# Second products three steps behind, each pass of a tile one tile later on ScalarE and VectorE, and an opening in single file

## The chip, the cores and the metric

The program runs on one core of a Trainium2 chip. The metric is the device time of one execution in microseconds (us); smaller is better. TensorE (PE) multiplies matrices into PSUM, ScalarE (ACT), VectorE (DVE) and GpSimd (POOL) work element by element, and SyncE (SP) issues most of the transfers. Each engine works through its own queue strictly in order, and engines meet only at semaphores.

## What is computed

The input is `x`, 4 sequences of 4096 tokens with 192 channels in float32. A causal convolution of 7 taps, whose weights are a softmax per head of 24 channels, gives 16384 tokens of 192 channels. Two layers of the same shape follow:

```python
x = attn_out.reshape(B * S, D)                 # after the convolution: 16384 x 192
h = x @ w_in;  g = h * np.cos(h);  x = g @ w_out      # first layer, 192 -> 2048 -> 192
h = x @ w_in2; g = np.where(h > 0, h, np.exp(np.minimum(h, 0)) - 1)
return g @ w_out2                                     # second layer
```

The weights of both layers arrive as float64 and are turned into pairs of 32-bit numbers on the chip, a high part and a low part; so are `x` and `g`. A product of two such pairs takes three products (high with high, low with high, high with low).

## The kernel before, in words

The tokens are cut into 32 blocks of 512. The unit of work is a step `(m, b, j)`: layer m, block b, and the j-th of 8 slices of 256 hidden channels. A step has two tiles, t = 2s and 2s + 1, each 128 hidden channels by 512 tokens. There are 512 steps. Blocks go in groups of four: 32 steps of the first layer for four blocks, then 32 of the second for the same four, eight times over.

Per step, TensorE does the first products of step s (`products_A`, 9 per tile, into a PSUM bank called `u`) and the second products of an earlier step s - LAG (`products_B`, 10 per tile, into the banks `acc`). Each uses half of the array's rows, and two run side by side: one stream is the 9 of the even tile and then 10 second products, the other 10 second products and then the 9 of the odd tile. So a step is 19 such pairs. While the second layer's weights are still being decoded, the second products of a step are 10 products on the whole array instead (`whole_B`), after the 9 pairs of first products; they need two `acc` banks and not four.

Between the two products each tile passes through the other engines: `emit_act1` (ACT reads `u`), `emit_mid` (DVE, first layer only), `emit_act2` (ACT, sine or exponential), `emit_g` (DVE, the last to read `u`, whose bank is then free), `emit_hi` (ACT, tile `gh`) and `emit_lo` (POOL, or DVE for odd tiles of the second layer, tile `gl`). `step(s)` writes these out by hand: each engine's queue has the order in which `step` calls them. The `u` banks form a ring: three while the weights are decoded, four afterwards.

At the end of a block, `half_evac` copies two of the four `acc` banks out on ACT and adds the other two on DVE (the next block's second products need the same banks), and `sums` finishes the block a piece at a time. `convs` gives one DVE instruction of a later block's convolution per half step of the second layer.

The opening is different. Weights are decoded by `decode` in four stages (load; ACT; DVE; POOL, then ACT and POOL once more), and `advance` moves pieces from stage to stage between the other instructions. All pieces use one PSUM bank, `brink`. The first two blocks go through the first layer side by side in 16 steps, block 1 two slices behind block 0 (SKEW); then come blocks 2 and 3.

Of the kernel before, what the change touches and what calls it, by code (L numbers as in the profile page):

```python
# [18 lines left out]
P = 128  # L19
# [4 lines left out]
SKEW = 2  # L24
LAG = 2
PAIR = 4
AWAKE = 14
RAW1, RAW2 = 4, 2
# [5 lines left out]
def conv_then_two_mlps(ctx, tc, x, weight, w_in1, w_out1, w_in2, w_out2, out):  # L34
# [40 lines left out]
    brink = ps_w.tile([P, N], F32, tag="t", name="t")  # L75
# [67 lines left out]
    zturn = {1: deque(range(ZN)), 2: deque(range(2, ZN))}  # L143

    def raw_tile(m):

        zturn[m].rotate(-1)
        t = zt.tile([P, 2 * N], I32, tag=f"zp{zturn[m][0]}", name="raw")
        return t.rearrange("p (n two) -> p n two", two=2)
# [7 lines left out]
    def decode(m, load, n):  # L157
# [5 lines left out]
        raw = raw_tile(m)[:, 0:n]  # L163
# [3 lines left out]
        t = brink[:, 0:n]  # L167
# [4 lines left out]
        size = w if scalar[0] else t  # L172
# [110 lines left out]
    XPS = {("a", 0): ("u0", "u1"), ("c", 0): ("u2", "b0"), ("c", 1): ("u0", "u1")}  # L283
# [4 lines left out]
    def bank(tag, name):  # L288
        return (ps_u if tag[0] == "u" else ps_a).tile([P, N], F32, tag=tag, name=name)
# [10 lines left out]
    def from_rows(what, b):  # L300
# [11 lines left out]
        ps = [bank(k, "xps") for k in XPS.get((what, b), ("b0", "b1"))]  # L312
        for o, k0, c, np in ((ps[0], KM, KH, 2 * Q), (ps[1], 0, KM, P)):
            cols = o[:, 0:np * c].rearrange("p (a k i) -> p k i a", k=c, i=Q)
            for k in range(c):
# [6 lines left out]
                nc.tensor.transpose(cols[0:D2, k], t[0:np, b % 2, k0 + k, P:D], ident[0:np, 0:np])  # L322
        yield
        H0 = HALO * Q
# [17 lines left out]
    def conv(what, b):  # L342
# [13 lines left out]
        o = yp.tile([P, N], F32, tag="y" + what, name="y", bufs=4 if what == "a" else 2)  # L356
# [103 lines left out]
    def split(b):  # L460
        if ("c", b) in ys:
            yield from split_pair(b)
        sh, sl, ch, cl = doubles(("sh", "sl")) + ready_x.pop(b) if b < 2 else doubles()
# [54 lines left out]
    def products_A(t):  # L518
# [4 lines left out]
        ops = [(k, w, h) for k in "cos" for w, h in (("h", "h"), ("l", "h"), ("h", "l"))]  # L523
# [17 lines left out]
    def whole_B(s):  # L541

        m, b, j = steps[s]
        if j == 0:
            acc[m, b] = [bank(f"{'ab'[b]}{k}", "acc") for k in (0, 1)]
# [9 lines left out]
    whole = {(1, 0), (1, 1)}  # L555
# [57 lines left out]
    def emit_hi(t):  # L613
        gh = wk.tile([P, N], F32R, tag="gh", name="gh", bufs=4)
# [3 lines left out]
    def emit_lo(t):  # L618
        gl = wk.tile([P, N], F32R, tag="gl", name="gl", bufs=4)
# [11 lines left out]
    def whole_evac(m, b):  # L631
        yield
        yield
# [7 lines left out]
        lazy.append(whole_z(b, z, c, e))  # L641
        yield

    def whole_z(b, z, c, e):
        lo, hi = half
        nc.vector.scalar_tensor_tensor(out=e[2][lo], in0=c[lo], scalar=TWO_PI, in1=e[3][lo], op0=ALU.mult, op1=ALU.add)
# [6 lines left out]
    def half_evac(m, b):  # L653
# [9 lines left out]
        yield  # L663
# [62 lines left out]
    raws = {1: RAW1, 2: RAW2}  # L726

    def fetch():
        while todo and len(loaded) + sum(len(stages[k]) for k in "12") < raws[todo[0][1]] and (todo[0][1] == 1 or moved):
# [22 lines left out]
    def need(m, at, *kinds):  # L752
        while any(ready.get((k, m), 0) < at for k in kinds):
            advance()

    def convs():
        for b in range(2, NBLK):
# [4 lines left out]
            while b - 4 not in split_done and b >= 4:  # L762
# [6 lines left out]
    conved, split_done = set(), set()  # L769
# [12 lines left out]
    begin_at = {max(s - (AHEAD, AHEAD2)[m - 1], 2 * NP - SKEW - 1 + 2 * (b - 2)): (m, b) for (m, b), s in first.items() if (m, b) not in whole}  # L782
# [8 lines left out]
    def step(s):  # L791
        now = 0 <= s < total
        if now:
# [8 lines left out]
        if ends:  # L802
            m, b = steps[s - LAG][:2]
            while not prepared and (m, b) == (1, 2):
                advance()
            assert not lazy
            finish = evac(m, b)
# [4 lines left out]
        for i in (0, 1):  # L812
# [15 lines left out]
            if not (ends and i) and (now and not first_mlp or s > 3 and ROWS - 1 not in conved and (i or 2 not in conved)):  # L828
# [116 lines left out]
```

## Time and profile before

| | |
|---|---|
| median of 3 runs | 2437.54 us (2435.3 to 2440.31) |
| the profiled execution | 2437.8 us, of which the span from first to last instruction is 2436.1 us |
| PE busy, weight loads busy | 96%, 77% of the span |
| ACT, DVE, POOL busy | 79%, 69%, 50% |
| granted TensorE clock, mean | 0.986 of full speed |

Busy shares are means over the whole program. An opening of some 265 us, in which weights are decoded, is followed by a long part that repeats itself for each group of four blocks, so a stretch of each is to be looked at by itself. The end of a matmul is modelled; the starts of successive matmuls tell how fast TensorE really goes.

### The profile page before, as it was taken

The numbers are of one execution on the slowest core, as the hardware profiler recorded it, in microseconds if no ns is written. First come the engines' busy times: TensorE is split into PE (matmuls) and PEld (weight loads), VectorE is DVE, ScalarE is ACT, GpSimd is POOL, SyncE is SP. The second block draws the span as 40 slices with busy tenths as digits, with TensorE's granted clock in tenths as the row PEclk, the third lists the DMA queues.
The fourth block names the chain that finished last, engine by engine and source line by source line (L and its number), as shares of the span: only waits on it lengthen the run. The fifth ranks groups of instructions, "written<-read, shape, count | busy, mean of one in ns | idle before, by whom it ended". The sixth has DMA issues, their size and how long they took to land.

```text
span 2436.1 us, 49759 instructions
## 1 busy us (share of the span) xinstructions
PE 2327.4 (96%) x19414; PEld 1884.4 (77%) x19414; DVE 1682.3 (69%) x2573; ACT 1926.9 (79%) x3426; POOL 1221.0 (50%) x975
## 2 busy tenths in 40 slices
PE   6777999999999999999999999999999999999998
PEld 4556877778888788777887788878888778877886
DVE  5776777667776686766776677666767668666654
ACT  4666878888888878878888888888888887887886
POOL 3665533664346633565336653366434663356532
PEclk8898999999999999999999999999999999999999
DMA  4233132111331022210331113211123102211011
GB/s 105 61 79 72 30 65 57 39 27 31 61 61 36 18 58 54 40 38 17 66 60 43 36 24 67 54 34 27 37 54 61 36 19 54 49 33 45 19 36 27
DMA packets 278876, 111.27 MB, mean 46 GB/s; under 512 B 231536, under 2 KB 245872, under 8 KB 278640
## 3 DMA queue, kind: packets, MB, share of 16 engines
q1 hardware_dynamic: 278192, 107.70, 20.9%
q8 instruction: 152, 2.49, 0.4%
q14 instruction: 84, 0.69, 0.1%
q10 hardware_dynamic: 448, 0.39, 0.1%
HBM read 29.91 MB, written 12.58 MB: 17 GB/s over the span
## 4 chain that ended last, share of the span: by engine, by line
PE 46%; DVE 23%; ACT 22%; issue 6%; POOL 2%; DMA 1%; SPq 1%; DVEq 0%; ACTq 0%; POOLq 0%
PE acc L563 24%; PE u L563 23%; ACT w L601 7%; DVE w L609 6%; ACT gh L615 6%; DVE w L595 5%; ACT w L586 3%; DVE w L611 3%; DVE gl L622 2%; DVE e L658 2%; DVE y L363 1%; POOL gl L622 1%; ACT w L603 1%; ACT e L659 1%; ACT e L660 1%
## 5 line engine op out<-in xcount | busy, mean ns | idle before, releaser
L622 POOL TENSOR_TENSOR gl<-w,gh 128x512 fp32r<-128x512 f32 x768 | 995.4, 1297 | 1153.1 <-ACT gh L615 890.4
L563 PE MATMUL acc<-gh,wo_hl 64*128 64x512 f32 x3968 | 1231.4, 391 | 15.5 <-DVE e L658 13.6
L615 ACT ACTIVATE gh<-w 128x512 fp32r<-128x512 f32 x1024 | 646.9, 632 | 216.5 <-DVE w L609 121.7
L563 PEld LDWEIGHTS acc<-gh,wo_hl 64*128 64x128 f32 x3968 | 719.5, 185 | 101.2 <-DVE e L658 26.9
L563 PE MATMUL acc<-gl,wo_hl 64*128 64x512 f32 x1984 | 773.4, 391 | 14.5 <-POOL gl L622 12.8
L563 PE MATMUL acc<-gh,wo_s 64*128 64x512 f32 x1984 | 773.9, 391 | 12.3 <-DVE e L658 11.1
L563 PE MATMUL acc<-gl,wo_s 64*128 64x512 f32 x1984 | 770.5, 389 | 0.0
L563 PE MATMUL u<-ch,wi_c 64*128 64x512 f32 x2048 | 645.1, 396 | 45.0 <-DVE w L609 32.9
L563 PE MATMUL u<-sh,wi_o 64*128 64x512 f32 x2048 | 627.1, 391 | 0.0
L609 DVE TENSOR_TENSOR w<-u,w 128x512 f32<-128x512 f32 x512 | 353.9, 691 | 357.6 <-ACT w L601 354.7
L611 DVE SCALAR_TENSOR_TENSOR w<-w,u 128x512 f32<-128x512 f32 x512 | 349.4, 682 | 212.4 <-ACT w L603 211.5
L563 PEld LDWEIGHTS u<-ch,wi_c 64*128 64x128 f32 x2048 | 373.5, 185 | 95.5 <-DVE w L609 38.0
L563 PE MATMUL u<-z,wi_o 64*128 64x512 f32 x1536 | 430.6, 386 | 0.0
L563 PEld LDWEIGHTS acc<-gl,wo_hl 64*128 64x128 f32 x1984 | 365.4, 185 | 71.5 <-POOL gl L622 36.7
L563 PEld LDWEIGHTS acc<-gh,wo_s 64*128 64x128 f32 x1984 | 365.3, 184 | 69.7 <-DVE e L658 33.0
L563 PEld LDWEIGHTS u<-sh,wi_o 64*128 64x128 f32 x2048 | 376.6, 187 | 37.4
L601 ACT ACTIVATE w<-w 128x512 f32<-128x512 f32 x512 | 323.7, 632 | 94.4 <-DVE w L595 89.3
L563 PE MATMUL u<-cl,wi_c 64*128 64x512 f32 x1024 | 395.9, 391 | 0.5 <-DMA cl<-z 0.5
L563 PE MATMUL u<-sl,wi_o 64*128 64x512 f32 x1024 | 395.3, 390 | 0.0
L563 PEld LDWEIGHTS acc<-gl,wo_s 64*128 64x128 f32 x1984 | 365.3, 185 | 33.6
L595 DVE SCALAR_TENSOR_TENSOR w<-u,w 128x512 f32<-128x512 f32 x512 | 348.7, 681 | 50.5 <-ACT w L586 49.9
L588 ACT ACTIVATE w<-u 128x512 f32<-128x512 f32 x512 | 303.9, 594 | 98.7 <-PE u L563 91.1
(123 smaller groups left out, 3413.9 us busy)
## 6 DMA issues: line engine op xcount, KB each, us to landing
out_dram<-e SPq DMA_DIRECT2D x192, 64.0 KB, 2.0
xa<-in_x_dram SPq DMA_DIRECT2D x112, 88.0 KB, 2.9
sh<-z SPq DMA_DIRECT2D x64, 128.0 KB, 2.4
sl<-z SPq DMA_DIRECT2D x64, 128.0 KB, 2.5
ch<-z SPq DMA_DIRECT2D x64, 128.0 KB, 2.4
cl<-z SPq DMA_DIRECT2D x64, 128.0 KB, 2.3
sh<-xh SPq DMA_DIRECT2D x62, 128.0 KB, 2.4
sl<-xl SPq DMA_DIRECT2D x62, 128.0 KB, 2.3
```

The lines of the kernel that those rows point to most:

```text
L363: nc.vector.scalar_tensor_tensor(out=o, in0=i, scalar=w, in1=o, op0=ALU.mult, op1=ALU.add)
L563: nc.tensor.matmul(o, lhsT=lhsT, rhs=rhs, start=first, stop=final)
L586: nc.scalar.activation(out=w.bitcast(I32), in_=u, func=AF.Copy, bias=0.25)
L588: nc.scalar.activation(out=w, in_=u, func=AF.Relu, scale=-1.0)
L595: nc.vector.scalar_tensor_tensor(out=w, in0=u, scalar=0.25, in1=w.bitcast(I32), op0=ALU.add, op1=ALU.subtract)
L601: nc.scalar.activation(out=w, in_=w, func=AF.Sin, scale=6.283185)
L603: nc.scalar.activation(out=w, in_=w, func=AF.Exp, scale=-1.0)
L609: nc.vector.tensor_tensor(out=w, in0=u, in1=w, op=ALU.mult)
L611: nc.vector.scalar_tensor_tensor(out=w, in0=w, scalar=-1.0, in1=u, op0=ALU.add, op1=ALU.max)
L615: nc.scalar.activation(out=gh, in_=wrk[t], func=AF.Copy)
L622: eng.tensor_tensor(out=gl, in0=wrk.pop(t), in1=f32(own[0]), op=ALU.subtract)
L658: add = lambda o, a: nc.vector.scalar_tensor_tensor(out=o, in0=a, scalar=scale, in1=o, op0=ALU.mult, op1=ALU.add)
```

## The change

Second products run three steps behind the first ones (LAG 3; `gh` and `gl` have six buffers each and not four). In `step`, each half step now calls `act1` and `mid` for tile t, `act2` and `g` for tile t - 1, and `hi` and `lo` for tile t - 2; before it was t, t and t - 1. Both additions of `half_evac` stand ahead of the odd tile's passes.

In the opening the blocks go one after another, each 8 steps. The ring has four `u` banks from the start; decoding has two banks (`brink` of two); the second products of the first blocks use the two banks `a0` and `a1`, and `b0`, `b1` are taken where the two decoding banks were once decoding is over. Up to three pieces move per step in the first 8 steps, and one per step later; the first layer's input weights come earlier in the order. The number of raw buffers follows from which of the four blocks' `z` tiles are still unused. The convolution's result of a block goes into the tile that later holds that block's `zc`, so the convolution of block b waits until block b - 4 has been doubled (`double_z`).

```diff
-SKEW = 2
-LAG = 2
+LAG = 3
-    brink = ps_w.tile([P, N], F32, tag="t", name="t")
+    brink = [ps_w.tile([P, N], F32, tag=f"t{k}", name="t") for k in range(2)]
+    def free_raws():
+        return [k for k in range(ZN) if present[0] < (k + 1) * NP + LAG - 4]
...
-        t = brink[:, 0:n]
+        brink.reverse()
+        t = brink[0][:, 0:n]
...
-        o = yp.tile([P, N], F32, tag="y" + what, name="y", bufs=4 if what == "a" else 2)
+        o = zt.tile([P, N], F32, tag=f"zc{b % ZN}", name="y") if what == "a" else yp.tile([P, N], F32, tag="yc", name="y")
...
-            blocks = list(range(b0, b0 + size))
-            if not steps:
-                steps += [(m, b, j - b * SKEW) for j in range(NP + SKEW) for b in blocks[0:2] if 0 <= j - b * SKEW < NP]
-                blocks = blocks[2:]
-            steps += [(m, b, j) for b in blocks for j in range(NP)]
+            steps += [(m, b, j) for b in range(b0, b0 + size) for j in range(NP)]
-    ring = deque((ps_u, f"u{k}") for k in range(3))
+    ring = deque((ps_u, f"u{k}") for k in range(4))
-    whole = {(1, 0), (1, 1)}
+    whole = set()
     def products(s):
         now, then = 0 <= s < total, 0 <= s - LAG < total
+        if then and steps[s - LAG][2] == 0 and not late:
+            whole.add(steps[s - LAG][:2])
-        gh = wk.tile([P, N], F32R, tag="gh", name="gh", bufs=4)
+        gh = wk.tile([P, N], F32R, tag="gh", name="gh", bufs=6)
-        gl = wk.tile([P, N], F32R, tag="gl", name="gl", bufs=4)
+        gl = wk.tile([P, N], F32R, tag="gl", name="gl", bufs=6)
     def half_evac(m, b):
...
         add(e[0], a0)
-        yield
         add(e[2], a1)
...
-            while b - 4 not in split_done and b >= 4:
+            while b >= ROWS and b - ROWS not in doubled:
                 yield
     def step(s):
...
             next(finish, None)
             if 0 <= t - 1 < 2 * total:
-                emit_hi(t - 1)
-                emit_lo(t - 1)
-            if not prepared:
-                advance(("42", "31")[i])
-            if now:
-                emit_act2(t)
-                emit_g(t)
+                emit_act2(t - 1)
+                emit_g(t - 1)
+            if not prepared and (s < NP + 1 or i and s % NP < NP - 1):
+                advance()
+            if 0 <= t - 2 < 2 * total:
+                emit_hi(t - 2)
+                emit_lo(t - 2)
+            if i:
+                next(finish, None)
...
+        if s < NP and not prepared:
+            advance()
-        if prepared and len(ring) == 3:
+        if prepared and not late:
             brief.close()
             top.close()
-            ring.appendleft((ctx.enter_context(tc.tile_pool(name="ps_s", bufs=1, space=bass.MemoryType.PSUM)), "u3"))
+            late.append(ctx.enter_context(tc.tile_pool(name="ps_s", bufs=1, space=bass.MemoryType.PSUM)))
```

Line numbers in the rows of order below are those of each kernel's own file. First, VectorE's queue in the first layer, where a block ends, in the kernel before. L595 is `mid`, L609 is `g`, L658 the two additions; the number behind `w` or `u` tells one tile from another.

```order
L595 SCALAR_TENSOR_TENSOR w_17686<-u_17646,w_17686 128x512
L609 TENSOR_TENSOR w_17686<-u_17646,w_17686 128x512
L658 SCALAR_TENSOR_TENSOR e_17689<-acc_17210,e_17689 128x512
L595 SCALAR_TENSOR_TENSOR w_17701<-u_17667,w_17701 128x512
L658 SCALAR_TENSOR_TENSOR e_17690<-acc_17212,e_17690 128x512
L609 TENSOR_TENSOR w_17701<-u_17667,w_17701 128x512
```

The same place in the changed kernel, where L612 is `mid`, L626 is `g` and L675 the additions.

```order
L612 SCALAR_TENSOR_TENSOR w_17533<-u_17493,w_17533 128x512
L626 TENSOR_TENSOR w_17484<-u_17456,w_17484 128x512
L675 SCALAR_TENSOR_TENSOR e_17536<-acc_17073,e_17536 128x512
L675 SCALAR_TENSOR_TENSOR e_17537<-acc_17075,e_17537 128x512
L612 SCALAR_TENSOR_TENSOR w_17562<-u_17514,w_17562 128x512
L626 TENSOR_TENSOR w_17533<-u_17493,w_17533 128x512
```

Before, `g` of a tile follows `mid` of the same tile; now the `mid` of the next tile stands between them. Both additions now stand ahead of the odd tile's `mid`.

Second, ScalarE's queue in the same layer, three tiles of the kernel before. L586 is `act1`, L615 `hi`, L601 `act2` (the sine).

```order
L586 ACTIVATE w_17579<-u_17551 128x512
L615 ACTIVATE gh_17582<-w_17570 128x512
L601 ACTIVATE w_17579<-w_17579 128x512
L586 ACTIVATE w_17628<-u_17588 128x512
L615 ACTIVATE gh_17631<-w_17579 128x512
L601 ACTIVATE w_17628<-w_17628 128x512
```

And of the changed kernel, with L603 for `act1`, L618 for `act2` and L632 for `hi`.

```order
L603 ACTIVATE w_17417<-u_17377 128x512
L618 ACTIVATE w_17368<-w_17368 128x512
L632 ACTIVATE gh_17422<-w_17359 128x512
L603 ACTIVATE w_17426<-u_17398 128x512
L618 ACTIVATE w_17417<-w_17417 128x512
L632 ACTIVATE gh_17431<-w_17368 128x512
```

The sine of a tile stood two places behind its own `act1`, with `mid` on VectorE between them; now it stands behind the `act1` of the next tile, and `hi` one tile further back.

Third, VectorE's queue in the opening, with one piece of weights (L177, L180, L181), in the kernel before.

```order
L595 SCALAR_TENSOR_TENSOR w_818<-u_788,w_818 128x512
L177 SCALAR_TENSOR_TENSOR raw_661<-raw_661,t_94 128x512
L180 TENSOR_SCALAR t_94<-w_782 128x512
L181 TENSOR_SCALAR w_782<-t_94 128x512
L609 TENSOR_TENSOR w_818<-u_788,w_818 128x512
```

In the changed kernel a piece (L182, L185, L186) stands in this way between the tiles.

```order
L612 SCALAR_TENSOR_TENSOR w_620<-u_568,w_620 128x512
L626 TENSOR_TENSOR w_599<-u_567,w_599 128x512
L182 SCALAR_TENSOR_TENSOR raw_532<-raw_532,t_95 128x512
L185 TENSOR_SCALAR t_95<-w_611 128x512
L186 TENSOR_SCALAR w_611<-t_95 128x512
```

The piece stood between `mid` and `g` of one tile; now it stands behind the `g` of the tile before.

## Rows read from the trace of the kernel before

**Rows 1.** The page: span, and TensorE with its weight loads.
```profile
span 2436.1 us, 49759 instructions
PE 2327.4 (96%) x19414; PEld 1884.4 (77%) x19414; DVE 1682.3 (69%) x2573; ACT 1926.9 (79%) x3426; POOL 1221.0 (50%) x975
```

**Rows 2.** Busy times by stretch; columns as in the first line.
```profile
core 0: us, PE busy (x) PEld busy (x) DVE busy (x) ACT busy (x) POOL busy (x), PEclk, DMA share, GB/s
21.60:53.70 32.10, 16.63 (x52) 8.04 (x52) 17.98 (x37) 14.20 (x30) 10.34 (x13) 0.71 0.18 50
53.70:222.00 168.30, 127.65 (x642) 90.62 (x644) 119.62 (x179) 100.92 (x185) 105.66 (x86) 0.86 0.29 77
411.00:557.10 146.10, 142.52 (x1219) 115.40 (x1217) 98.19 (x150) 119.82 (x209) 93.83 (x74) 1.00 0.16 35
557.10:698.70 141.60, 139.88 (x1219) 116.52 (x1217) 105.43 (x161) 115.68 (x209) 51.06 (x40) 1.00 0.27 52
650.00:700.00 50.00, 50.00 (x442) 41.02 (x440) 33.54 (x52) 41.65 (x76) 16.80 (x13) 1.00 0.27 56
1350.00:1400.00 50.00, 48.29 (x415) 38.58 (x413) 33.59 (x52) 40.83 (x72) 32.72 (x26) 1.00 0.14 33
```

**Rows 3.** Line view: `act1` of the second layer, with first and last start.
```profile
L588 ACT ACTIVATE w<-u x512: 573/600/612, 267.3 to 2422.3; 128x512 f32<-128x512 f32 x171
```

**Rows 4.** Timeline: the end-of-block copy of the last blocks (start, length).
```profile
2359.61 0.59 ACT L659 ACTIVATE e<-acc 128x512 f32<-128x512 f32 x1
2394.34 0.59 ACT L659 ACTIVATE e<-acc 128x512 f32<-128x512 f32 x1
```

**Rows 5.** Timeline of the first layer: start, length, [idle before <-releaser].
```profile
1347.21 0.63 ACT L601 ACTIVATE w<-w 128x512 f32<-128x512 f32 x1
1347.32 1.30 POOL L622 TENSOR_TENSOR gl<-w,gh 128x512 fp32r<-128x512 f32 x1 [0.61 <-ACT gh L615]
...
1347.75 0.58 ACT L586 ACTIVATE w<-u 128x512 int32<-128x512 f32 x1
1347.88 0.69 DVE L609 TENSOR_TENSOR w<-u,w 128x512 f32<-128x512 f32 x1 [0.70 <-ACT w L601]
...
1348.48 0.68 DVE L595 SCALAR_TENSOR_TENSOR w<-u,w 128x512 f32<-128x512 f32 x1
...
1349.20 0.63 ACT L601 ACTIVATE w<-w 128x512 f32<-128x512 f32 x1
...
1349.86 0.69 DVE L609 TENSOR_TENSOR w<-u,w 128x512 f32<-128x512 f32 x1 [0.70 <-ACT w L601]
```

**Rows 6.** Waits, 411 to 557.1 us: total, times, longest.
```profile
DVE w L609 <- ACT w L601: 43.2, 59, 1.2
```

**Rows 7.** Costliest groups, 411 to 557.1 us: the additions at a block's end.
```profile
L658 DVE SCALAR_TENSOR_TENSOR e<-acc,e 128x512 f32<-128x512 f32 x8 | 5.4, 679 | 0.0
```

**Rows 8.** Waits, 100 to 222 us: TensorE's weight load before a first product.
```profile
PEld u L563 <- DVE w L609: 32.9, 12, 5.3
```

**Rows 9.** Costliest groups on DVE, 53.7 to 222 us: busy, mean ns.
```profile
L609 DVE TENSOR_TENSOR w<-u,w 128x512 f32<-128x512 f32 x39 | 26.7, 685 | 29.2 <-ACT w L601 29.2
...
L363 DVE SCALAR_TENSOR_TENSOR y<-xT,wch,y 128x512 f32<-128x512 f32 x18 | 17.2, 956 | 0.1
L181 DVE TENSOR_SCALAR w<-t 128x512 int32<-128x512 int32 x19 | 13.1, 691 | 1.2
L177 DVE SCALAR_TENSOR_TENSOR raw<-raw,t 128x512 int32<-128x512 int32 x19 | 12.8, 676 | 0.0
...
L181 DVE TENSOR_SCALAR w<-t 128x256 int32<-128x256 int32 x2 | 0.8, 424 | 0.2
```

**Rows 10.** The chain that ended last, in the opening: start, length, what.
```profile
120.28 3.65 PE u L563 x15
```

**Rows 11.** Timeline of the end: second products with nothing beside them.
```profile
2424.30 0.62 PE L563 MATMUL acc<-gh,wo_hl 64*128 64x512 f32 x4
...
2426.54 0.40 PE L563 MATMUL acc<-gl,wo_s 64*128 64x512 f32 x2
```

More of the change, by code (lines that the diff above doesn't have):

```diff
@@ L142, in conv_then_two_mlps, with raw_tile @@
     ZN = max(GROUPS)
[L143 to L148, printed above, removed]
+    zturn, present = deque(range(ZN)), [0]
+    def free_raws():
+        return [k for k in range(ZN) if present[0] < (k + 1) * NP + LAG - 4]
+    def raw_tile():
+        free = free_raws()
+        zturn.rotate(-1)
+        while zturn[0] not in free:
+            zturn.rotate(-1)
+        t = zt.tile([P, 2 * N], I32, tag=f"zp{zturn[0]}", name="raw")
         return t.rearrange("p (n two) -> p n two", two=2)
@@ L288, in bank @@
     def bank(tag, name):
-        return (ps_u if tag[0] == "u" else ps_a).tile([P, N], F32, tag=tag, name=name)
+        pool = ps_u if tag[0] == "u" else ps_a if tag[0] == "a" else late[0]
+        return pool.tile([P, N], F32, tag=tag, name=name)
     def starts():
@@ L311, in from_rows @@
         p = slice(0, D2 if alone else P)
-        ps = [bank(k, "xps") for k in XPS.get((what, b), ("b0", "b1"))]
-        for o, k0, c, np in ((ps[0], KM, KH, 2 * Q), (ps[1], 0, KM, P)):
+        H0 = HALO * Q
+        if b < 2:
+            ps = [bank(k, "xps") for k in XPS[what, b]]
+        for n, (k0, c, np, at) in enumerate(((KM, KH, 2 * Q, slice(0, H0)), (0, KM, P, slice(H0, NX)))):
+            o = ps[n] if b < 2 else ring_bank("xps")
             cols = o[:, 0:np * c].rearrange("p (a k i) -> p k i a", k=c, i=Q)
@@ L322, in from_rows @@
                 nc.tensor.transpose(cols[0:D2, k], t[0:np, b % 2, k0 + k, P:D], ident[0:np, 0:np])
+            if b > 1:
+                nc.scalar.activation(out=xT[:, at], in_=o[:, 0:np * c], func=AF.Copy)
+                if n == 0:
+                    yield
+        if b > 1:
+            xTs[what, b] = xT
+            return
         yield
-        H0 = HALO * Q
         if b == 0:
@@ L460, in split @@
     def split(b):
-        if ("c", b) in ys:
+        if b >= 2 and ("c", b) in ys:
             yield from split_pair(b)
-        sh, sl, ch, cl = doubles(("sh", "sl")) + ready_x.pop(b) if b < 2 else doubles()
+        sh, sl, ch, cl = doubles(("sh", "sl")) + ready_x.pop(b, [None] * 2) if b < 2 else doubles()
         if b >= 2:
@@ L544, in whole_B @@
         if j == 0:
-            acc[m, b] = [bank(f"{'ab'[b]}{k}", "acc") for k in (0, 1)]
+            acc[m, b] = [bank(k, "acc") for k in ("a0", "a1")]
         o, c = acc[m, b]
@@ L631, in whole_evac @@
     def whole_evac(m, b):
-        yield
-        yield
+        for _ in range(3):
+            yield
         a, c = acc.pop((m, b))
@@ L725, in conv_then_two_mlps @@
     loaded, stages = deque(), {k: deque() for k in "1234"}
-    raws = {1: RAW1, 2: RAW2}
     def fetch():
-        while todo and len(loaded) + sum(len(stages[k]) for k in "12") < raws[todo[0][1]] and (todo[0][1] == 1 or moved):
+        while todo and len(loaded) + sum(len(stages[k]) for k in "12") < len(free_raws()) and (todo[0][1] == 1 or moved):
             next(todo[0][3])
@@ L753, in need @@
         while any(ready.get((k, m), 0) < at for k in kinds):
+            assert loaded or any(stages.values())
             advance()
@@ L767, in convs @@
             conved.add(b)
-    conved, split_done = set(), set()
+    conved, split_done, doubled = set(), set(), set()
     cq = convs()
@@ L781, in conv_then_two_mlps @@
             first[m, b] = s
-    begin_at = {max(s - (AHEAD, AHEAD2)[m - 1], 2 * NP - SKEW - 1 + 2 * (b - 2)): (m, b) for (m, b), s in first.items() if (m, b) not in whole}
+    begin_at = {s - ((AHEAD, AHEAD2)[m - 1] if (m, b) != (1, 2) else 3): (m, b) for (m, b), s in first.items() if (m, b) not in ((1, 0), (1, 1))}
     chores, lazy = deque(), deque()
@@ L802, in step @@
         if ends:
-            m, b = steps[s - LAG][:2]
-            while not prepared and (m, b) == (1, 2):
-                advance()
             assert not lazy
-            finish = evac(m, b)
+            finish = evac(*steps[s - LAG][:2])
         if s in begin_at:
@@ L853, in opening @@
         conved.update((0, 1))
-        advance()
         yield
-        tokens("a", 2)
-        tokens("c", 2)
-        advance()
-        yield
-        tokens("a", 3)
-        moved.add(True)
-        yield
+        for what, b in (("c", 2), ("a", 2), ("a", 3)):
+            yield from from_rows(what, b)
+            if b == 3:
+                moved.add(True)
+            yield
     with tc.manual_schedule():
```

82 lines of the change are left out of this document (38 added, 44 removed).

## The prediction

> **What bounds the kernel now.** I read the page first: TensorE is busy for 2327.4 of 2436.1 us [rows 1], which looks like a kernel with 109 us left to take. The stretches [rows 2] say otherwise. Between 650 and 700 us TensorE runs 442 matmuls, between 1350 and 1400 only 415, and both count as almost wholly busy. So I count starts and not busy time. 442 matmuls are 221 side-by-side pairs, 0.2262 us each; a step of 19 pairs then needs 4.30 us and a block of 8 steps 34.4 us. That is the floor of this order of work.
>
> How far above it is the kernel? The second layer's `act1` first starts at 267.3 us, for the first tile of step 32, and last at 2422.3 us, for the last tile of step 511 [rows 3]. Its products of 9 pairs (2.04 us) come before it, so step 32 begins near 265.2 us, and 480 steps take 2422.2 - 265.2 = 2157 us: 35.95 us per block, 1.55 us above the floor, 93 us in 60 blocks. The opening does 32 steps in 265.2 us where the floor is 138 us. These two hold all there is to gain: about 220 us at most.
>
> The repeating part loses most in the first layer: 146.1 us for four blocks [rows 2], 36.5 us each. The timeline [rows 5] shows why. ACT's sine (L601) starts at 1347.21, DVE's `g` (L609) waits 0.70 us for it and starts at 1347.88, then comes `mid` (L595) at 1348.48, the next sine at 1349.20, the next `g` at 1349.86. `g`, `mid` and sine form a ring over two engines: 0.69 + 0.68 + 0.63 us, 1.98 us per tile, of TensorE's 2.15 us. The 0.17 us left, 2.7 us per block, must hold everything that a block's end puts into either queue, the two additions of 0.68 us each [rows 7] first of all. It cannot, so the first layer runs at this ring's pace. `g` waits for the sine 59 times there, 43.2 us in all [rows 6].
>
> In the opening the longest wait of TensorE is for `g` to free a `u` bank: 32.9 us between 100 and 222 us, 12 times, up to 5.3 us [rows 8]. No engine is full: DVE 119.6 of 168.3 us, 71% [rows 2]. Three banks and a decoding piece between `mid` and `g` of one tile set the pace.
>
> **The change, part by part.** *One tile later.* The sine of t - 1 now follows `act1` of t, and its `mid` was finished a half step ago; `g` of t - 1 follows `mid` of t, and `hi` takes a `g` from the half step before. No instruction needs the result of the one just issued on the other engine, and the ring is open. What is left is throughput: ACT three times 0.63 us = 1.9 us, DVE two times 0.69 = 1.4 us per 2.15 us [rows 5]; POOL one of 1.30 us. ACT's extra work in a first-layer block is some 5 instructions, 3 us, against 16 times 0.25 = 4 us of room. All three fit.
>
> *What it costs.* A bank is held longer. Before, `g` came some 2.8 us after the tile's products (0.58 + 0.68 + 0.63 + 0.69 and three hand-overs). Now it waits for the next tile's products, `act1` and `mid`: 2.15 + 0.58 + 0.68 + 0.69 and two hand-overs, 4.2 us. The bank is needed again four tiles later: a step is 4.30 us, products take 2.04 us, so 2 x 4.30 - 2.04 = 6.57 us are allowed, and 2.3 us remain. The two additions take 1.36 us of these, a convolution tap about 0.75 us; both together still fit. The second products ask for `gh` three steps later, 9.7 us after an odd tile's products, and `hi` ends at about 6, `lo` at 7.4 us; the longer lag covers the later order. Six buffers of `gh`, `gl` cover three steps.
>
> *Block ends.* Both additions now run before the odd tile's `mid`, so `acc` is free 1.4 us after the last second product; the stream that needs it starts 2.04 us after. I cost this at nothing; with the cover gone it would be 1 us per block.
>
> *Convolution into `zc`.* A tap now waits for the transfers out of `zc` of block b - 4. Those are issued three steps before that block; the taps of odd blocks come 3 steps or more later. No cost; a late one would use DVE's spare time first.
>
> So a block comes to between 34.4 us and 34.7 us, the spacing of the last blocks of before (2359.61 to 2394.34 [rows 4]), which have no convolution beside them and where TensorE ends last. I take 34.65 us, nearest to that row: 60 x 34.65 = 2079 us instead of 2157. Above it, 35.2 us if half the loss remains.
>
> *The opening.* Before, two blocks share each piece of weights; now block 0 alone meets the whole first-layer decoding, some three pieces per step, and DVE is the fullest there. From its first `mid`, put at 24 us (before, the first products begin at 21.6 us, where the first stretch [rows 2] begins), to the last `mid` of step 4 the changed queue has 10 `mid` and 8 `g` (18 x 0.69 = 12.4 us), 14 pieces of three or four instructions, 8 of them 256 wide at 0.43 us and 6 of 512 at 0.69 us [rows 9], 26.6 us with gaps, and 4.4 us for block 1's convolution and split: 43.4 us. At DVE's share of before, 71%, this is 61 us, so step 5 begins near 85 us; at a full DVE 67 us, at the 56% of the stretch from 21.6 to 53.7 us [rows 2] 101 us. Then 27 steps: 12 carry a piece of the second layer, where DVE has 4 x 0.69 + 2.06 + about 0.9 us for a tap [rows 9] = 5.7 us, about 5.6 us a step; 15 carry none, 4.45 us; three block ends of 1 us: 137 us. Step 32 begins at 222 us, and the bounds are 67 + 15 x 4.30 + 12 x 5.5 = 198 us and 101 + 137 = 238 us.
>
> *The end.* Three steps of second products stand alone and not two: one more of 10 pairs, 2.3 us (2424.30 to 2426.54 [rows 11]), on top of the 13.9 us from 2422.2 to the span's end.
>
> The sum: 222 + 2079 + 13.9 + 2.3 = 2317 us of span, and with the 1.7 us that the execution takes beside its span 2319 us. The profiled execution (2437.8 us) is as long as the median (2437.54), so nothing is to be corrected.
>
> [...]
>
> **Rivals.** *The gain goes half way.* The ring is open, but another wait takes its place at each block's end (the additions wait for the last second product, with `g` queued behind them, and ACT's copies come late). For it: 141.6 us for four blocks of the second layer before [rows 2], 35.4 us each, without a `mid` in the ring. Against it: 2.3 us of room. 222 + 60 x 35.2 + 17.9 = 2352 us.
>
> *Busy time was true.* Only idle time of TensorE goes: 2327.4 + 1.7 = 2329 us. Against it stand 415 and 442 matmuls in nearly equal busy time; its time lies in the forecast's own range, and it has no chance of its own.
>
> [...]
>
> *Banks held too long: slower.* If `g` comes more than 6.57 us after a tile's products, TensorE waits for a bank in every step. Two steps then last 2.04 us and this delay x, a step (2.04 + x) / 2. It decides from x = 7.15 us on: a step of 4.59 us, 222 + 480 x 4.59 + 17.9 = 2443 us, the time of before. With x = 7.25 us it is 2470 us. For it: 4.2 + 1.36 + 0.75 + 0.69 (an odd `lo` on DVE) = 7.0 us where all meet. Against it: they meet once per block and not in every step.
>
> **How the numbers follow.** The forecast has 0.70 (2319 us, its own range 2290 to 2342), half way 0.17, the low clock 0.07, banks held too long 0.06. The opening's bounds move the time by -24 and +16 us, the block's by -15 and +4; leaving out the last two cases the range is 2285 to 2362 us. A difference of 0.2% (5 us) is what a measurement of this kernel can tell. Faster 0.93, same 0.01, slower 0.06.
>
> **What would show it.** Right: 438 or more matmuls in any 50 us of the repeating part, in both layers; `g` no longer waiting for the sine by 0.70 us; block ends 34.5 to 34.8 us apart; TensorE's wait for `g` in the opening mostly gone; the second layer's first `act1` near 224 us. Wrong: first-layer blocks of 36 us (the ring was not the cause), waits of `u` for `g` throughout (banks), or `act1` of the second layer after 250 us (the opening).

## Result and the profile after

The changed kernel takes 2375.23 us (median of 4 runs, 2373.47 to 2376.2), the kernel before on the same chip 2438.46 us: a ratio of 0.9741, 95% interval 0.9724 to 0.9758. The forecast was 2319 us with a range of 2285 to 2362: the direction is right, and 56 us of the expected gain are missing.

The page of the changed kernel, its first lines, answering to [rows 1]:

```profile
span 2371.8 us, 49445 instructions
...
PE 2287.8 (96%) x19254; PEld 1847.0 (78%) x19254; DVE 1832.1 (77%) x2566; ACT 1867.8 (79%) x3435; POOL 1247.8 (53%) x973
```

TensorE is 96% busy as before. VectorE is the one to look at: it has about as many instructions as before and 150 us more busy time. Three stretches of the repeating part, columns as in [rows 2]: a second layer with convolutions beside it, the first layer behind it, and 50 us of that one:

```profile
1092.50:1238.00 145.50, 141.57 (x1230) 114.33 (x1228) 123.96 (x162) 114.58 (x210) 55.97 (x41) 1.00 0.29 56
1238.00:1374.60 136.60, 136.60 (x1208) 112.88 (x1208) 100.65 (x149) 113.22 (x208) 93.29 (x72) 1.00 0.15 32
1300.00:1350.00 50.00, 50.00 (x444) 41.34 (x442) 35.42 (x55) 40.16 (x75) 36.92 (x29) 1.00 0.19 44
```

The first layer runs at the floor: 444 matmuls in 50 us, where there were 415. The second layer, which had 141.6 us for four blocks (1219 matmuls), now has 145.5 (1230 matmuls), or 144.3 us between the block ends below. The copies at block ends (timeline of ScalarE, start and length) show it block by block, as in [rows 4]:

```profile
1069.12 0.59 ACT L676 ACTIVATE e<-acc 128x512 f32<-128x512 f32 x1
1103.57 0.59 ACT L676 ACTIVATE e<-acc 128x512 f32<-128x512 f32 x1
...
1141.77 0.59 ACT L676 ACTIVATE e<-acc 128x512 f32<-128x512 f32 x1
...
1177.67 0.59 ACT L676 ACTIVATE e<-acc 128x512 f32<-128x512 f32 x1
...
1213.31 0.59 ACT L676 ACTIVATE e<-acc 128x512 f32<-128x512 f32 x1
1247.87 0.59 ACT L676 ACTIVATE e<-acc 128x512 f32<-128x512 f32 x1
```

34.45 us for the last block of the first layer, then 38.20, 35.90 and 35.64 us for the three second-layer blocks that have a convolution beside them, then 34.56.

The ring is open. VectorE's timeline in the first layer, for [rows 5], and its waits over four blocks (1238 to 1374.6 us), for [rows 6]:

```profile
1301.99 0.69 DVE L612 SCALAR_TENSOR_TENSOR w<-u,w 128x512 f32<-128x512 f32 x1 [0.39 <-ACT w L603]
1302.60 0.68 DVE L626 TENSOR_TENSOR w<-u,w 128x512 f32<-128x512 f32 x1
1304.00 0.69 DVE L612 SCALAR_TENSOR_TENSOR w<-u,w 128x512 f32<-128x512 f32 x1 [0.72 <-ACT w L603]
```

```profile
DVE w L612 <- ACT w L603: 30.6, 40, 1.1
DVE w L626 <- ACT w L618: 4.4, 5, 1.3
```

`g` (L626) follows `mid` (L612) without a pause and waits for the sine 5 times, 4.4 us, where it was 59 times, 43.2 us. VectorE now waits for `act1`, so for TensorE's products.

In the second layer what is left stands at the block's end. First TensorE's wait for the additions in the kernel before (411 to 2340 us), where both layers had it:

```profile
PE acc L563 <- DVE e L658: 21.7, 47, 1.4
```

Then TensorE's waits in the changed kernel from 393 to 2320 us, three for the additions in each group of four blocks, and VectorE, GpSimd and TensorE around one block's end (timeline):

```profile
PE acc L578 <- DVE e L675: 15.9, 18, 1.0
PE u L578 <- DMA ch<-z: 2.1, 3, 0.9
PE u L578 <- DMA cl<-z: 1.9, 5, 0.4
```

```profile
1143.47 0.69 DVE L628 SCALAR_TENSOR_TENSOR w<-w,u 128x512 f32<-128x512 f32 x1 [1.06 <-ACT w L620]
1144.02 1.29 POOL L639 TENSOR_TENSOR gl<-w,gh 128x512 fp32r<-128x512 f32 x1 [4.04 <-ACT gh L632]
1144.08 1.78 DVE L379 SCALAR_TENSOR_TENSOR y<-xT,wch,y 128x512 f32<-128x512 f32 x1
1145.78 1.27 DVE L675 SCALAR_TENSOR_TENSOR e<-acc,e 128x512 f32<-128x512 f32 x2
...
1146.52 0.50 PE L578 MATMUL acc<-gh,wo_hl 64*128 64x512 f32 x1 [0.97 <-DVE e L675]
```

A convolution tap (L379) stands in VectorE's queue right ahead of the two additions (L675), and takes 1.78 us beside GpSimd's `lo` (L639). TensorE waits 0.97 us for the additions. The other two waits of the group are of the same kind. The one at the end of the group's last first-layer block is 0.98 us, behind a tap of 1.74 us. The one a block later than that shown is 0.70 us, behind the first tap of another convolution, which is a plain product (L377, 0.46 us where nothing disturbs it):

```profile
1179.92 1.29 POOL L639 TENSOR_TENSOR gl<-w,gh 128x512 fp32r<-128x512 f32 x1 [3.99 <-ACT gh L632]
1179.98 1.52 DVE L377 TENSOR_SCALAR y<-xT,wch 128x512 f32<-128x512 f32 x1
1181.42 1.27 DVE L675 SCALAR_TENSOR_TENSOR e<-acc,e 128x512 f32<-128x512 f32 x2
```

The costliest groups of VectorE (before from 411 to 2422 us, then the changed kernel from 393 to 2356 us) say how common the long taps are. A tap takes 1155 ns on average where it took 785, the cast of z 2036 where it took 814, and the addition, which reads PSUM, 679 as ever:

```profile
L363 DVE SCALAR_TENSOR_TENSOR y<-xT,wch,y 128x512 f32<-128x512 f32 x210 | 164.8, 785 | 0.0
```

```profile
L379 DVE SCALAR_TENSOR_TENSOR y<-xT,wch,y 128x512 f32<-128x512 f32 x216 | 249.5, 1155 | 0.0
...
L675 DVE SCALAR_TENSOR_TENSOR e<-acc,e 128x512 f32<-128x512 f32 x112 | 71.5, 679 | 0.0
L693 DVE CAST z<-e 128x512 fp32r<-128x512 f32 x28 | 57.0, 2036 | 0.0
```

The opening is the second place. `act1` of the second layer, for [rows 3]:

```profile
L605 ACT ACTIVATE w<-u x512: 573/600/611, 250.6 to 2356.2; 128x512 f32<-128x512 f32 x171
```

Step 32 begins near 250.6 - 2.1 = 248.5 us (forecast 222), the 60 blocks take 2356.1 - 248.5 = 2107.6 us (the last tile is counted from 0.1 us ahead of its `act1`, as in the prediction), 35.13 us each (forecast 34.65), and 15.7 us follow (forecast 16.2). The two misses, 26.5 and 28.6 us, are the whole of it. The prediction's own sign for the first, `act1` of the second layer after 250 us, has come true. From step 5 on five steps of the opening (13, 14, 18, 19 and 26) take 8.9 to 12.0 us; in the last three of them ScalarE stands still (its timeline):

```profile
167.66 0.63 ACT L487 ACTIVATE xh<-y 128x512 fp32r<-128x512 f32 x1 [4.22 <-DVE y L379]
...
181.25 0.63 ACT L178 ACTIVATE t<-raw 128x512 f32<-128x512 uint32 x1 [5.28 <-DMA raw<-in_moe_w_in_dram]
...
221.37 0.62 ACT L178 ACTIVATE t<-raw 128x512 f32<-128x512 uint32 x1 [3.65 <-DMA raw<-in_moe_w_in_dram]
```

### The profile page after: what moved, and what is told of

Its sections match the earlier page's. It is cut to its first block, busy times and chain, and to the rows that moved or that the text cites. A ratio compares the mean times of both kernels' runs of the same rounds, so it can differ in the third digit from the quotient of the medians.

```text
span 2371.8 us, 49445 instructions
## 1 busy us (share of the span) xinstructions
PE 2287.8 (96%) x19254; PEld 1847.0 (78%) x19254; DVE 1832.1 (77%) x2566; ACT 1867.8 (79%) x3435; POOL 1247.8 (53%) x973
## 4 chain that ended last, share of the span: by engine, by line
PE 84%; DVE 6%; ACT 3%; issue 2%; DMA 2%; POOL 1%; SPq 1%; ACTq 0%; DVEq 0%; POOLq 0%
PE acc L578 42%; PE u L578 40%; DVE y L379 2%; PE acc L568 2%; DVE w L628 1%; DMA raw<-in_moe_w_in_dram 1%; ACT w L605 1%; DVE e L675 1%; DMA cl<-z 1%; ACT w L620 1%; DVE y L377 1%; DVE w L612 0%; DVE w L626 0%; ACT e L676 0%; ACT e L677 0%
## 5 line engine op out<-in xcount | busy, mean ns | idle before, releaser
L639 POOL TENSOR_TENSOR gl<-w,gh 128x512 fp32r<-128x512 f32 x768 | 1014.0, 1321 | 1067.4 <-ACT gh L632 813.0
L578 PE MATMUL acc<-gh,wo_hl 64*128 64x512 f32 x3840 | 1177.1, 387 | 18.2 <-DVE e L675 17.5
L578 PEld LDWEIGHTS acc<-gh,wo_hl 64*128 64x128 f32 x3840 | 701.9, 184 | 100.4 <-DVE e L675 26.0
L578 PE MATMUL acc<-gh,wo_s 64*128 64x512 f32 x1920 | 742.1, 388 | 0.0
L578 PE MATMUL acc<-gl,wo_s 64*128 64x512 f32 x1920 | 741.4, 387 | 0.0
L578 PE MATMUL acc<-gl,wo_hl 64*128 64x512 f32 x1920 | 739.1, 386 | 0.0
L632 ACT ACTIVATE gh<-w 128x512 fp32r<-128x512 f32 x1024 | 640.9, 626 | 15.4 <-DVE w L628 13.8
L578 PE MATMUL u<-ch,wi_c 64*128 64x512 f32 x2048 | 623.5, 394 | 17.9 <-DVE w L626 15.1
L578 PE MATMUL u<-sh,wi_o 64*128 64x512 f32 x2048 | 611.1, 387 | 0.0
L612 DVE SCALAR_TENSOR_TENSOR w<-u,w 128x512 f32<-128x512 f32 x512 | 352.0, 688 | 273.9 <-ACT w L603 270.2
L603 ACT ACTIVATE w<-u 128x512 int32<-128x512 f32 x512 | 305.9, 598 | 198.0 <-PE u L578 183.8
L578 PEld LDWEIGHTS acc<-gh,wo_s 64*128 64x128 f32 x1920 | 352.2, 184 | 42.8 <-DVE e L675 6.2
L626 DVE TENSOR_TENSOR w<-u,w 128x512 f32<-128x512 f32 x512 | 348.6, 681 | 43.5 <-ACT w L618 43.5
```

The costliest lines, as they stand in the source:

```text
L578: nc.tensor.matmul(o, lhsT=lhsT, rhs=rhs, start=first, stop=final)
L603: nc.scalar.activation(out=w.bitcast(I32), in_=u, func=AF.Copy, bias=0.25)
L612: nc.vector.scalar_tensor_tensor(out=w, in0=u, scalar=0.25, in1=w.bitcast(I32), op0=ALU.add, op1=ALU.subtract)
L626: nc.vector.tensor_tensor(out=w, in0=u, in1=w, op=ALU.mult)
L632: nc.scalar.activation(out=gh, in_=wrk[t], func=AF.Copy)
L639: eng.tensor_tensor(out=gl, in0=wrk.pop(t), in1=f32(own[0]), op=ALU.subtract)
```

## Experiments

All edits are of the changed kernel. Intervals are those of the ratio to the kernel before.

**e4: the order alone undone.**

```diff
-  emit_act2(t - 1); emit_g(t - 1); ...; emit_hi(t - 2); emit_lo(t - 2)
+  emit_hi(t - 1); emit_lo(t - 1); ...; emit_act2(t); emit_g(t)
```

> Undoes one part: in each half step hi, lo of tile t - 1 and then sine (exp) and g of tile t again, as before; the longer lag, single file, decoding and convolution stay as changed. Theory (the ring of g, mid and sine was what held the first layer, and the later order alone opens it): first-layer blocks back at 36.3 to 36.8 us, 28 of them x 2 us = 57 us lost; second-layer blocks 35.2 to 35.5 us with taps near 0.8 us, 10 us won; 2420 us (2405 to 2435). Rival (the gain of the repeating part comes from the lag and the freed additions and not from the order): first-layer blocks stay at 34.5, 2365 to 2380 us.

2432.02 us, 0.997 (0.996 to 0.9981). First-layer blocks are back at 35.8 to 37.0 us, and the ring's wait with them (VectorE, 403 to 552 us); taps are back at 763 ns (393 to 2356 us):

```profile
DVE w L626 <- ACT w L618: 47.3, 64, 1.2
```

```profile
L379 DVE SCALAR_TENSOR_TENSOR y<-xT,wch,y 128x512 f32<-128x512 f32 x216 | 164.7, 763 | 0.0
```

Undoing the later order loses 57 us, some 10 of them in the opening (the second layer's first `act1` starts at 261.0 us); without it all other edits together bring 7 us. And the same taps are quick when the order puts GpSimd's `lo` elsewhere. Quick taps alone do not free the block ends: in e4 TensorE waits 22.2 us for the additions and 15.1 us for ScalarE's copies (393 to 2320 us).

**e1: six of the seven taps left out. e2: no `lo` on VectorE. e3: taps only in the second half of a step.**

```diff
 e1   for k in range(K):
+         if k and b >= ROWS: yield; continue
 e2-  eng = nc.vector if t % 2 and prepared and steps[t // 2][0] == 2 else nc.gpsimd
 e2+  eng = nc.gpsimd
 e3-  next(cq, None)                                # one tap in each half
 e3+  for _ in range((1 - i) if ends else 2 * i): next(cq, None)
```

> Leaves out, from block 4 on, six of the seven taps of each convolution on VectorE (the transposes, the first tap and all transfers stay), so the output is not the reference's. Theory A (the second layer loses 5.7 us per group because taps on VectorE are stretched by GpSimd's instructions, from 0.79 to 1.16 us, and fill VectorE): all blocks 34.4 to 34.5 us apart, 7 x 5.7 = 40 us gone: 2335 us (2330 to 2345). Theory B (the second layer loses by the transfers at a block's start, which stand in SP's queue behind the load of x that waits for the transpose, whatever the taps do): first blocks of a group stay at 37 us and more, 2360 us or above. Theory C (banks are held too long in the later order): no change, 2370 us or above.

> The odd lo of the second layer goes to GpSimd as well, so VectorE has g and a tap per tile and no lo; GpSimd has two lo per step. Theory A (VectorE is full: 0.68 + 1.16 + 0.37 us per tile of 2.15): 0.37 us less per tile, the taps still stretched (1.1 to 1.4 us), blocks 34.5 to 34.8 us: 2340 us (2335 to 2352). Theory A with GpSimd as the next bound (two lo of 1.3 to 1.75 us, and the sums, in 4.3 us): about as now, 2365 to 2385. Theory B (transfers): 2372 to 2378. Theory C (banks held): 2372 to 2378.

> The same taps, but both of a step in its second half, where lo is VectorE's own, and none in the first half, where GpSimd does lo. Theory A (what stretches a tap is GpSimd's lo at the same time): mean tap 0.80 to 0.95 us, blocks with a convolution 34.5 to 35.2 us, 2350 us (2338 to 2362). Rival (the amount of work on VectorE, wherever it stands, is what costs): the mean tap unchanged at 1.1 us or more, 2370 us or above; later if g of the next step now waits behind two taps.

e1: 2344.64 us, 0.9615 (0.9596 to 0.9635); taps cost 31 of the 40 us that theory A gave them, and theory C falls. Theory B seems to fall too, as the first blocks of a group are 34.4 us apart; but e6 below shows that with the taps in place the transfers cost 20 us. One block per group stays at 35.6 us in e1: there the first tap, which e1 keeps, stands right ahead of the additions and takes 1.52 us, and TensorE waits 0.69 us, six times from 393 to 2320 us:

```profile
PE acc L581 <- DVE e L678: 4.2, 6, 0.7
```

e2: 2382.01 us, 0.9766 (0.975 to 0.9782), no faster than the changed kernel though VectorE is spared 256 instructions. Taps are longer still, and TensorE's wait for the additions has not moved (393 to 2356 and 393 to 2320 us):

```profile
L379 DVE SCALAR_TENSOR_TENSOR y<-xT,wch,y 128x512 f32<-128x512 f32 x216 | 316.0, 1463 | 0.0
```

```profile
PE acc L578 <- DVE e L675: 16.1, 18, 1.0
```

e3: 2392.29 us, 0.9806 (0.9789 to 0.9823). The mean tap fell to 989 ns, not as far as the 0.80 to 0.95 us of theory A, and the time rose. In a block's last step my edit left the tap in the first half, and there it still takes 1.78 us, right ahead of the additions, for which TensorE still waits 14.8 us (393 to 2320 us). What the further 17 us are is open: TensorE's waits in that stretch add up to 23.0 us where they were 20.4.

```profile
1153.57 1.78 DVE L379 SCALAR_TENSOR_TENSOR y<-xT,wch,y 128x512 f32<-128x512 f32 x1
1155.27 1.28 DVE L675 SCALAR_TENSOR_TENSOR e<-acc,e 128x512 f32<-128x512 f32 x2
```

So theory A ("VectorE is full") was wrong as put: less work on VectorE (e2) and a shorter mean tap (e3) did not help. What is left to test is the one tap per block that stands ahead of the additions.

**e5: no tap in a block's last step. e12: the tap stays, GpSimd's `lo` beside it goes to VectorE behind the additions.**

```diff
 e5-  if not (ends and i) and (...): next(cq, None)
 e5+  if not (ends and (i or prepared)) and (...): next(cq, None)
 e12     if i:
             next(finish, None)                     # the additions
 e12+        if ends and ...: emit_lo(t - 3, True)  # on VectorE
 ...
 e12-    emit_lo(t - 2)
 e12+    if not (ends and not i and ...): emit_lo(t - 2)
```

> The same taps, but none in a step whose end is a block's end (before, one stood there in VectorE's queue right ahead of the two additions, 1.78 us long beside GpSimd's lo). Theory A2 (not the load of VectorE as such, but this one stretched tap per block makes the additions late, and TensorE waits 0.97, 0.97 and 0.70 us for them in each group): these three waits go, with a few tenths for the slow first products behind each: 7 x 2.7 to 3.0 us = 19 to 21 us, 2355 us (2350 to 2360); what stays is the first block's 1.3 us for the transfers. Rival (VectorE is full in the second layer, so a tap placed elsewhere makes the next block's additions late as well): 2366 to 2376 us.

> Only the even lo of the second-layer step in which a block ends moves: from GpSimd, where it ran beside the tap ahead of the additions, to VectorE behind the additions. The tap stays where the changed kernel has it. Theory A2 (that tap takes 1.78 us and not 0.74 because GpSimd's lo runs beside it, and by these 1.04 us the additions are late): the three waits of 0.97, 0.97 and 0.70 us per group go, 7 x 2.7 = 19 us, 2357 us (2351 to 2363), as without the tap. Rival (any tap at that place makes the additions late, stretched or not): at least half of the waits stays, 2365 to 2376 us.

e5: 2358.07 us, 0.9661 (0.9646 to 0.9675). e12: 2353.8 us, 0.9641 (0.9627 to 0.9656). In e12 the tap stands where it stood and takes 0.75 us; the additions start 0.67 us after it and not 1.70, and of TensorE's waits from 393 to 2320 us those for the additions are gone (its timeline, then the waits):

```profile
1134.49 0.75 DVE L379 SCALAR_TENSOR_TENSOR y<-xT,wch,y 128x512 f32<-128x512 f32 x1
1135.16 1.28 DVE L675 SCALAR_TENSOR_TENSOR e<-acc,e 128x512 f32<-128x512 f32 x2
```

```profile
PE u L578 <- DMA ch<-z: 2.6, 4, 1.2
PE u L578 <- DMA cl<-z: 2.5, 6, 0.4
```

Two different edits, one of which leaves the tap and adds work to VectorE, take away the same waits. What made the additions late was the stretch of this one tap.

**e6: e5, and z doubled four steps ahead.**

```diff
-AHEAD, AHEAD2 = 6, 3
+AHEAD, AHEAD2 = 6, 4
```

> The edit of the run before and, beside it, the doubled z of a second-layer block issued four steps ahead and not three, so that its transfers no longer stand in SP's queue behind the load of x that waits for VectorE's transpose. Theory (these transfers cost 0.86 + 0.42 us once per group): 9 us less than the run before, 2346 us (2341 to 2351). Rival (they are hidden once the additions come on time): the same as the run before, within 3 us.

2338.01 us, 0.9579 (0.9564 to 0.9593): 20 us less than e5, not 9. From the second on, blocks are 34.4 to 34.6 us apart, and no wait of TensorE is left from 393 to 2320 us, while the mean tap is still 1108 ns (393 to 2356 us). The 20 us are more than the waits. In e5 TensorE waits for z's transfers at one place in each of six groups, where the second block of the second layer begins, 10.4 us in all (393 to 2320 us), and these six blocks are 18.4 us longer than 34.45 us each. In two of the six, slow products followed (stretches of e5 around waits of 1.68 and 0.42 us; columns as in [rows 2]):

```profile
1126.00:1128.00 2.00, 1.24 (x6) 0.83 (x8) 1.89 (x4) 0.42 (x1) 0.00 (x0) 0.80 0.71 164
1128.00:1130.00 2.00, 2.00 (x12) 1.52 (x10) 0.00 (x0) 0.00 (x0) 0.00 (x0) 0.50 0.00 0
1130.00:1132.00 2.00, 2.00 (x16) 1.59 (x16) 0.00 (x0) 1.17 (x3) 0.00 (x0) 0.85 0.00 0
1132.00:1134.00 2.00, 2.00 (x20) 1.66 (x18) 1.95 (x2) 1.24 (x3) 1.30 (x1) 1.00 0.00 0
```

The granted clock falls to 0.50, and 12 matmuls run in 2 us where two stretches later 20 do. This block lost 4.4 us for 2.1 us of waits, and the other of the two 4.6 us. Around the longest waits of the remaining four, 1.76 and 0.42 us, the granted clock stayed at 1.00:

```profile
567.00:569.00 2.00, 1.11 (x8) 0.66 (x10) 1.93 (x4) 0.46 (x1) 0.00 (x0) 1.00 0.78 179
569.00:571.00 2.00, 2.00 (x20) 1.67 (x18) 0.00 (x0) 0.46 (x1) 0.00 (x0) 1.00 0.00 0
```

These four lost 0.8 us each beyond their waits, for a reason that no run shows.

**e7: one tap of seven for blocks 2 and 3 in the opening. e8: decoding last in a half step.**

```diff
 e7   for k in range(K):
+         if k and b < ROWS: yield; continue
 e8-  advance(); emit_hi(t - 2); emit_lo(t - 2); next(finish, None)
 e8+  emit_hi(t - 2); emit_lo(t - 2); next(finish, None); advance()
```

> Leaves out, for blocks 2 and 3 alone, six of the seven taps of each convolution on VectorE, so the output is not the reference's. Theory O1 (the long steps 13, 14 and 18 of the opening, 12.0, 8.9 and 10.8 us, come from left-over taps that the split of blocks 2 and 3 forces into VectorE's queue at once): these steps fall to 5 to 7 us, step 32 begins 11 to 15 us earlier, 2362 us (2357 to 2366). Rival O2 (decoding sets the pace of the opening, whatever stands beside it): step 32 begins within 4 us of now, 2371 to 2377 us.

> While weights are decoded, the decoding piece stands behind hi, lo and the block end's copies of a half step and not ahead of them. Theory O3 (in steps 19 and 26, 10.8 and 11.0 us long, ScalarE waits 5.28 and 3.65 us for a piece's raw weights with the block end's copies queued behind, and TensorE then waits 5.2 and 5.1 us for acc): the copies no longer wait, 5 to 10 us less, 2367 us (2363 to 2371). Rival (each piece now comes a little later, and the products wait for their weights or the raw weights arrive later): 2375 to 2385 us.

e7: 2364.18 us, 0.9689 (0.9675 to 0.9704), 11 us less; steps 13 and 14 fall from 12.0 and 8.9 to 6.7 and 6.6 us, step 18 only from 10.8 to 9.6. e8: 2378.32 us, 0.9745 (0.9729 to 0.9762), no gain; steps 19 and 26 are 10.6 and 9.8 us: the wait for raw weights (5.33 and 3.23 us on ScalarE) holds the next `act1` in place of the copies.

**e9, e10, e11, on top of e6: x for block 4 loaded later; taps of the opening earlier; both.**

```diff
 e9   if b == ROWS:
+         while not prepared: yield
          load_a(ROWS); load_c(ROWS)
 ...
 e10- s > NP - 3 and ... and (i or s >= NP and 2 not in conved)
 e10+ s > NP - 4 and ... and (i or 2 not in conved)   # and block 3 split 4 steps ahead
```

> The kernel without a tap in a block's last step and with z doubled four steps ahead, and beside it the load of x for block 4 put behind the decoding (step 32 and not step 18). Theory O4 (in step 19 ScalarE waits 5.28 us for raw weights because their load stands in SP's queue behind eight loads of x, 4.4 us): step 19 falls from 10.8 to about 6.5 us, 2334 us (2331 to 2336). Rival (SP's queue waits there for block 3's split anyway): 2336 to 2340 us.

> The kernel without a tap in a block's last step and with z doubled four steps ahead, and beside it the opening's convolutions begun earlier (both halves of a step from step 5 on and not one half from step 6) and block 3's split four steps ahead and not six, so that fewer taps are left over to be forced at once. Theory O1 (forced left-over taps cost 7 to 9 us in steps 13 and 14 and some in 18): steps 13 and 14 fall to about 7 us each, the steps 5 to 12 grow by some 3 us together: 2331 us (2327 to 2335). Rival (VectorE has no room in steps 5 to 12 either, each tap lengthens its step by its own 0.8 to 1.3 us): 2336 to 2342 us.

> Both edits of the opening together with the two of the repeating part. Theory (the causes add): the two gains of the runs beside it add, 2327 us (2322 to 2332). Rival (they share one wait): no better than the better of the two.

e9: 2331.81 us, 0.9552 (0.9538 to 0.9567); step 19 falls from 10.8 to 7.3 us: the raw weights did stand behind the loads of x. e10: 2338.04 us, no change: steps 13 and 14 fall to 6.7 and 6.3 us, 8 us together, and steps 6, 7 and 12 grow to 7.6, 7.0 and 8.0, 5 us together. The rest is lost in steps 19 to 21, where ScalarE waits up to 7.29 us for raw weights. The rival holds for the larger part: moved taps lengthen the steps that they move to. e11: 2332.86 us, no better than e9.

**e13: e9 with the copies at the opening's block ends earlier. e14: that with one opening tap of seven.**

```diff
 e13-    for _ in range(3): yield      # whole_evac
 e13+    for _ in range(2): yield
```

> The kernel with x for block 4 loaded late (run e9), and beside it the copies that end blocks 0 to 2 in the opening one place earlier in both queues: behind mid of the step's second tile and not behind the sine, g, a decoding piece, hi and lo as well. Theory O5 (TensorE waits 11.4 us in three places for acc in the opening, since a whole block has one pair of banks and the next block's second products need them at once; the copies are late because ScalarE stands in front of a missing tap or raw weights): 4 to 9 us less, 2325 us (2322 to 2329). Rival (ScalarE and VectorE are held by the same missing tap or load wherever the copies stand, or g comes later by them): 2330 to 2335 us.

> The run beside it, without six of the seven taps of blocks 2 and 3, so the output is not the reference's. If the miss of the opening (step 32 at 248 us and not at 222) is the sum of taps, raw weights behind loads of x and late copies at block ends, taps take 11 to 13 us more off: 2313 us (2309 to 2318), with step 32 at 224 to 229 us. If something else sets the opening's pace (decoding on VectorE, the clock), step 32 stays above 232 us: 2319 us or above.

e13: 2330.89 us, 0.9561 (0.9546 to 0.9575), as e9, although TensorE's wait for `acc` between 80 and 250 us fell from 11.4 to 2.8 us; its wait for `u` rose from 12.9 to 17.3 us. O5 falls: that wait went along with others. e14: 2316.15 us, 0.9501 (0.9485 to 0.9517), with

```profile
L608 ACT ACTIVATE w<-u x512: 573/599/610, 231.4 to 2298.4; 128x512 f32<-128x512 f32 x171
```

step 32 at 229 us, at the edge of what the first theory allowed, and the opening still slower than forecast although 18 of its 21 taps are left out.

e9 is the best of the kernels that compute everything, e13 its equal: 2331 to 2332 us, 43 us below the changed kernel.

## Why the prediction was wrong

*The floor and the ring: right.* Blocks without a stall are 34.39 to 34.56 us apart, and in e6 all are 34.37 to 34.60 us apart from the second on. That the ring held the first layer, e4 shows from the other side. The weight loads' busy time did not tell how near a stretch was to the floor: from 1300 to 1350 us it is 41.34 of 50 us with 444 matmuls in the changed kernel, and in e6 it is all of the 50 us with 445:

```profile
1300.00:1350.00 50.00, 50.00 (x445) 50.00 (x443) 39.26 (x57) 41.18 (x77) 37.50 (x29) 1.00 0.14 33
```

*Banks: right.* From 393 to 2320 us TensorE waits 0.5 us in all for `g` of the changed kernel; the 2.3 us of room were there.

*The step that failed: "Block ends ... I cost this at nothing".* I counted the additions from the last second product, as if nothing stood ahead of them in VectorE's queue. In the second layer a tap does. I had priced a tap at 0.75 us, from an order in which GpSimd's `lo` ran at another time; the new order lets `hi` and `g` start behind the same exponential, `lo` behind `hi` and the tap behind `g`, so the two meet, and the tap takes 1.78 us. Undisturbed it is harmless (e12); stretched, it makes TensorE wait 0.7 to 1.0 us, three times a group, 17 to 21 us in all (e5, e12). The blocks that have nothing but such a wait are 1.1 to 1.4 us longer, near the 1 us that I had named as the price of a lost cover.

The traces show what I did not weigh: the tap beside `lo` takes 0.74 + 1.04 us, and the changed kernel's 120 additions, which have one input in PSUM, take 0.67 to 0.69 us each, beside GpSimd's instructions too. The tap uses nothing of `lo`, and its row shows no wait ahead of it: here two engines meet without a semaphore between them. Where the tap starts first, it is `lo` that takes longer, 1.82 us and not 1.30 (timeline of the changed kernel):

```profile
589.63 0.74 DVE L379 SCALAR_TENSOR_TENSOR y<-xT,wch,y 128x512 f32<-128x512 f32 x1
589.71 1.82 POOL L639 TENSOR_TENSOR gl<-w,gh 128x512 fp32r<-128x512 f32 x1 [0.55 <-ACT gh L632]
```

*"Convolution into zc ... No cost": wrong in a way I did not look at.* z's transfers, issued three steps ahead, stand behind a load of x that waits for VectorE's transpose (1120.23 us; load at 1121.16, transfers 1123.25 to 1128.39). I checked the time of issue and not what stands ahead in SP's queue. The load stood there in the kernel before as well. For the same block, the last of these transfers was issued 5.2 us ahead of the block's first `act1` before; now it is 3.7 us, and TensorE waits 0.86 and 0.42 us. With e5's edit made, this was worth 20 us (e6).

*The rival "half way"* had 35.2 us per block against 35.13 measured, and the place, the additions at the block's end. Its reason, ScalarE's copies coming late, was wrong: they end at 1142.85, 2.9 us ahead of the additions. Its time of 2352 us was low because it took the opening at 222 us.

*The opening, the second step that failed: "27 steps ... 137 us".* The first half was right: step 5 was due at 85 us, and its `act1` starts at 79.1. The 27 steps behind it take 171 us and not 137, so this term of the sum was 34 us too small. The runs show a part of this. The load of x ahead of raw weights cost 6 us (e9). Taps cost 11 to 15 us (e7, e14), of which I had 12 x 0.9 = 11 us in the sum, so they explain 4 us of the miss at most (the trace has 18 taps there and not 12, 1346 ns each on average). Without taps the sum would be 126 us, and e14, with one tap of seven and without that load, still takes 151.5 us (79.9 to 231.4): some 25 us stay open. There ScalarE waits 9.9 us for raw weights, and steps 5 to 7 take 5.7 to 5.8 us each where I had 4.45, with the transposes of blocks 2 and 3 on TensorE, which I had not counted. Whether these two are the rest was not tried. No run shows these steps held at a low clock, to which the forecast gave 0.07: from 79 to 250 us the granted clock was 0.92 in the changed kernel, which is an estimated 0.08 x 171 = 14 us at most, and 0.97 in e14. TensorE's weight loads still wait 21.8 us for `g` from 80 to 250 us, which I had said would mostly go. I had added up each engine's work and charged almost no wait between in-order queues.

## What to carry to other kernels

When an order is changed, work out anew which instructions of VectorE and GpSimd start together, and take VectorE's durations from a place where GpSimd is busy beside it: the tap had 0.74 us alone and 1.78 us beside `lo`. Then look at what stands directly ahead of the one instruction that TensorE waits for: average load and mean durations told little here (e2, e3, e6), one instruction's place told 20 us. What stands ahead of a transfer in its queue counts (3.7 us ahead of the block's first `act1` and not 5.2), and a pause of TensorE of 2.1 to 2.2 us in e5 cost more than its length: 4.4 us where the clock fell behind it, 3.0 us where it did not.

## What was not expected of the hardware

- A tap of 0.74 us took 1.72 to 1.80 us beside a GpSimd `lo` of 1.3 us that had started 0.05 to 0.12 us earlier; one that started 0.57 us behind `lo` took 1.28 us. Both end 0.55 us behind `lo`, which fits a wait for the other's end and not a slower pace. Forms stretched so, by their means: tap, cast of z (2036 ns for 814 before), `xl` (1407 for 682). Not stretched: those with an input in PSUM (678 to 688), and VectorE's transposes (700).
- Behind a pair of waits of 1.68 and 0.42 us in e5 the granted clock fell to 0.50 for 2 us (1128 to 1130 us); behind a pair of 1.76 and 0.42 us (569 to 571 us) it stayed at 1.00, as it did in the changed kernel behind the wait of 0.97 us at a block's end (1146 to 1150 us).
